# The MLP's up and down weight tiles in alternation, in a fused attention, MoE and MLP kernel on one Trainium2 core

## The chip, the core and the metric

The kernel is one launch on 1 core of a Trainium2 chip. A core has TensorE (PE, with its weight loads PEld), VectorE (DVE), ScalarE (ACT), GpSimd (POOL) and a queue for DMA issues, SyncE (SP). Each engine works through its own list of instructions in order, and waits on the others by semaphores. The metric is the device time of one execution in microseconds; it is given as the median of several runs.

## The reference

Attention with a learned position bias, then a mixture of experts with a capacity, then a dense MLP. Only the last concerns the change:

```
def _moe2_ref(x, w_in, w_out):          # x 1152x512, w_in 512x2048, w_out 2048x512
    h = x @ w_in
    g = np.maximum(0.01 * h, h)
    return (g @ w_out).astype(np.float32)

def reference(**kwargs):
    attn_out = _attn_ref(**attn_kwargs)
    B, H, S, D = attn_out.shape
    x = np.ascontiguousarray(attn_out.transpose(0, 2, 1, 3)).reshape(B * S, H * D)
    x = _moe_ref(x=x, **moe_kwargs)     # tokens over an expert's capacity give zero rows
    return _moe2_ref(x=x, **moe2_kwargs)
```

The weights `w_in` and `w_out` come as 64-bit floats.

## The kernel before

Attention runs first, unit by unit, then the routing, the experts (`big_step`, `small`) and last the dense MLP (`chunk`), which the change is about. In the runs here `chunk` is called once, as `chunk(0, True)`: 608 columns (tokens) in five groups of up to 128. A branch behind it holds further chunks.

**The weights.** The MLP's weights are 16 tiles of 128 x 1024: tiles 0 to 7 are the up matrix, 256 hidden units each, tiles 8 to 15 the down matrix, 256 hidden units each. Down tile 8+j needs the hidden units of up tile j. `PO` is the order in which the loop takes them; I call an index into it a place. Before, it is four up tiles, four down, four up, four down; the last three places, 13 to 15, are worked token group by token group behind the loop, each group's output being scaled and scattered when it is done (`emit`).

**Conversion.** A tile arrives as 64-bit floats (`conv_load`, 1 MB into a buffer `w`) and is made into a 32-bit tile `raw` by three passes on VectorE (`conv_op`, lines 689, 691 and 693), each of 128 x 1024. The passes of all tiles from place 3 on are one generator, `convs`; the loop pulls them with `next(cv, None)` at set points, and after a third pass the load of the tile two places on is issued. The tiles of the first three places are converted earlier: `conv_drip` does it inside the attention, and their results go to memory (`wsc`) and are fetched again during the experts (`DSL`).

**Splitting.** For precision each operand is a high and a low part. `wsplit` makes them from `raw`: a cast on ScalarE (line 675) and a subtraction on GpSimd (line 676, on VectorE for the last tile). At the start of place i the loop splits the tile of place i+2. A product is three matmuls.

**An up tile** (`up_half`, four times): 12 matmuls of 304 columns into one of three `g` buffers in PSUM; ScalarE's `mul` by 0.01 (line 884); VectorE's max of that and the `g` buffer (line 885), after which the buffer is free; then, called for the half before, the copy of the high part on ScalarE (line 892) and its residual on VectorE (line 893), in `split_h`. The hidden activations are `hq`.

**A down tile**: five groups of three matmuls of 512 columns, twice (`down_tok`), which is 30 matmuls into five `ac` accumulators. `split_h` is called for each first group, so that the pending last half of the up tile before is finished there. Passes are pulled at the points `DCV`.

The order of the work on each engine is the order of this code; no scheduler changes it.

Of the kernel before, what the change touches and what calls it, by code (L numbers as in the profile page):

```python
# [41 lines left out]
MOF = (0, 608)  # L42
NMC = len(MCS)
DCV = (0, 2, 4, 1)
PO = (0, 1, 2, 3, 8, 9, 10, 11, 4, 5, 6, 7, 12, 13, 14, 15)
MC = max(MCS)
XW = T + CAPB
SR1 = S + CAPB
# [26 lines left out]
def tile_attention_moe_mlp(ctx, tc, qc, kc, vc, wpk, cst, ctok, cap, wm, wo, out):  # L75
# [126 lines left out]
    def tick(k=1):  # L202
        for _ in range(k):
            while dq:
                try:
                    next(dq[0])
                    break
                except StopIteration:
                    dq.pop(0)
# [276 lines left out]
    def route_acc(b, cs):  # L486
        for c in cs:
            a = b * NCH + c
            nc.vector.tensor_tensor(out=acc[:, a + 1], in0=acc[:, a], in1=oh[:, b, c], op=ALU.add)
            yield  # L490
# [70 lines left out]
    def run(gen):  # L561
        for _ in gen:
            pass

    def scatter(b, c):
        n = 128 if c < NFULL else TAIL
        nc.gpsimd.indirect_dma_start(srt, bass.IndirectOffsetOnAxis(slots[b][0:n, c : c + 1].bitcast(U32), 0), xns.pop((b, c))[0:n], None,
                                     bounds_check=SROWS - 1, oob_is_err=False)
# [99 lines left out]
    raws, Ps, xhls, regs = [], [], [], {}  # L668
    PE, ACT, DVE, SP = ET.PE, ET.Activation, ET.DVE, ET.SP

    def wdma(src, raw):
        nc.sync.dma_start(raw, src)

    def wsplit(raw, P_, eng):
        nc.scalar.copy(P_[:, 0], raw)  # L675
        eng.tensor_tensor(out=P_[:, 1], in0=raw, in1=P_[:, 0].bitcast(F32), op=ALU.subtract)  # L676

    wsc = dr.tile([16, 128, 1024], F32, name="wsc")
    cvl = {}

    def conv_load(q, w64):
        cvl[q] = w64.bitcast(U32)
        nc.sync.dma_start(w64, wo[q].bitcast(I32).rearrange("p (f t) -> p f t", t=2))

    def conv_op(q, dst, i):
        o = dst.bitcast(U32)
        hi, lo = cvl[q][:, :, 1], cvl[q][:, :, 0]
        if i == 0:
            nc.vector.tensor_scalar(o, hi, 3, 0x3FFFFFFF, op0=ALU.logical_shift_left, op1=ALU.bitwise_and)
        elif i == 1:  # L690
            nc.vector.scalar_tensor_tensor(out=o, in0=hi, scalar=0xC0000000, in1=o, op0=ALU.bitwise_and, op1=ALU.bitwise_or)
        else:
            nc.vector.scalar_tensor_tensor(out=o, in0=lo, scalar=29, in1=o, op0=ALU.logical_shift_right, op1=ALU.bitwise_or)  # L693
# [3 lines left out]
            conv_op(q, dst, i)  # L697

    CV0 = 20
    CVA = [0, 1, 2]  # L700
    cvd = {}

    def g_w64(k):
        conv_load(CVA[k], wp.tile([128, 1024, 2], I32, name="w64g", tag="G", bufs=3))

    def conv_drip(n, slot):
        k, odd = divmod(n - CV0, 2)
        if not 0 <= k < len(CVA):
            return
# [3 lines left out]
        if i < 3:  # L713
            conv_op(CVA[k], cvd[k], i)
            tick()

    def wsrc(e, j):
        return wm[bass.ds(e, 1), j].rearrange("a p f -> p (a f)")
# [45 lines left out]
    def hooks(n):  # L764
# [28 lines left out]
        k, odd = divmod(n - CV0 - 2, 2)  # L793
        if odd == 0 and 0 <= k < len(CVA):
            nc.sync.dma_start(wsc[CVA[k]], cvd[k])
            if k + 3 < len(CVA):
                g_w64(k + 3)
# [24 lines left out]
    def tail_part(fa):  # L822
        att.close()
        mo = ctx.enter_context(tc.tile_pool(name="mo", bufs=1))
        spare = wp.tile([128, 1024], F32, name="spare", tag="bs", bufs=5)
# [28 lines left out]
        def hg(part, m, lo, n):  # L854
            o = MC * (m % 4) + lo
            return hq[2 * part + m % 8 // 4][:, o : o + n]
# [32 lines left out]
        def split_h():  # L889
            if gfh:  # L890
                gf, m, lo, n = gfh.pop()
                nc.scalar.copy(hg(0, m, lo, n), gf)  # L892
                nc.vector.tensor_tensor(out=hg(1, m, lo, n), in0=gf, in1=hg(0, m, lo, n).bitcast(F32), op=ALU.subtract)  # L893
# [13 lines left out]
        def yprep(c):  # L907
            n = MCS[c] // 2
            for lo in (0, n):
                for k in range(NP):  # L910
                    yk = y[:, k, MOF[c] + lo : MOF[c] + lo + n]
                    h = yhl[:, 0, k, lo : lo + n]
                    nc.scalar.copy(h, yk)
                    nc.vector.tensor_tensor(out=yhl[:, 1, k, lo : lo + n], in0=yk, in1=h.bitcast(F32), op=ALU.subtract)
# [64 lines left out]
        def list1():  # L979
            yield from route1b()  # L980
            yield from totals(1)
            yield from blocklist()
# [3 lines left out]
        def bval(l, i, f, engines):  # L986
            o = 3 * (NLST * l + i) + (2, 0, 1)[f]
            return nc.values_load(blk[0:1, o : o + 1], engines=engines, min_val=0, max_val=(E_N - 1, SROWS - CAPB, T - 1)[f])
# [3 lines left out]
        def load_x(base):  # L992
            for t, n in xtiles:
                nc.sync.dma_start(xr[t][0:n], srt[sl_(base + 128 * t, n), 0:DM])
# [4 lines left out]
        def load_xs(base):  # L999
            nc.sync.dma_start(xsr, srt[sl_(base, CAPS), 0:DM])  # L1000
# [13 lines left out]
        DSL = (3, 7, 12)  # L1014
        DSS = (4, 11)

        def post0(j, mm):
            s = 2 * j + mm
            if s == 0:
                run(fin_c(*fa))  # L1020
                run(route_acc(1, [NFULL]))
                scatter(1, 2)
            if s == 1:
                scatter(1, 3)
            if s == LS:
                nxt["g"] = list1()
            for _ in range(LN if s >= LS else 0):
                next(nxt["g"], None)
            if s == LE:
                run(nxt["g"])  # L1030
            if s < 2:
                wdma(wsrc(regs["e0"], 6 + s), R8[6 + s])
            if s in DSL:
                wdma(wsc[DSL.index(s)], spare)
            if s in DSS:
                wsplit(spare, Ds[DSS.index(s)], nc.vector)
            if s in (6, 8, 10, 12):
                nc.scalar.copy(y[:, s // 2 - 3], pre[:, 0:480].unsqueeze(1).to_broadcast([128, 3, 480]))
            if s == LE + 1:
                nxt["e"] = bval(0, 1, 0, [SP])  # L1040
            if s == LX:
                load_x(bval(0, 1, 1, [SP]))
                load_xs(bval(1, 0, 1, [SP]))
            for q in NXQ.get(s, ()):
                wdma(wsrc(nxt["e"], q), R8[q])
# [132 lines left out]
        def conv_start(i):  # L1178
            if i < 16:
                conv_load(PO[i], w64s[i % 2])  # L1180

        def convs():
            for i in range(3, 16):
                for o in range(3):
                    conv_op(PO[i], raws[i % 4], o)
                    if o == 2:
                        conv_start(i + 2)
                    yield
# [19 lines left out]
        def chunk(c, first):  # L1208
            w = MCS[c]
            groups = [(t, min(128, w - 128 * t)) for t in range(-(-w // 128))]  # L1210
            cv = convs()
            PP = [Ds[i] if first and i < 2 else Ps[i % 4] for i in range(16)]
            if not first:
                for i in range(3):
                    wdma(wsc[i], raws[i])
                yprep(c)
            for i in range(3, 5):
                conv_start(i)
            if not first:
                for i in range(2):  # L1220
                    wsplit(raws[i], PP[i], nc.vector)
            for i in range(13):
                if i + 2 < 16:
                    wsplit(spare if first and i == 0 else raws[(i + 2) % 4], PP[i + 2], nc.gpsimd)
                q = PO[i]
                if q < 8:
                    for g in (0, 2, 1, 3):
                        up_half(PP[i], 2 * q + g // 2, w // 2 * (g % 2), w // 2)
                        if g != 3:
                            next(cv, None)  # L1230
                else:
                    for kk in range(2):
                        for t, n in groups:
                            down_tok(PP[i], 2 * (q - 8) + kk, t, n)
                            if t == 0:
                                split_h()
                            if 2 * t + kk in DCV:
                                next(cv, None)
                if i == 5:
                    for t, n in groups:  # L1240
                        nc.sync.dma_start(idg[0:n, t], sid[MOF[c] + 128 * t : MOF[c] + 128 * t + n].bitcast(I32))
            wsplit(raws[15 % 4], PP[15], nc.vector)
            for t, n in groups:
                for i in range(13, 16):
                    for kk in range(2):
                        down_tok(PP[i], 2 * (PO[i] - 8) + kk, t, n)
                emit(t, n)
# [121 lines left out]
```

## Time and profile before

| | |
|---|---|
| median of 3 runs | 410.69 us (410.64 to 411.08) |
| the profiled execution | 410.08 us |
| its span in the trace | 408.2 us |
| TensorE busy | 377.8 us, 93% |
| VectorE busy | 308.3 us, 76% |
| ScalarE busy | 241.1 us, 59% |
| GpSimd busy | 139.3 us, 34% |
| mean granted clock of TensorE | 0.988 |

The span is the time from the first to the last instruction in the trace; the execution's own time is 1.9 us longer. Busy time is summed over the whole span and says nothing about which engine sets the pace of one stage. The ends of matmuls are modelled, so how fast TensorE goes is read from the starts of its matmuls.

### The profile page before, as it was taken

Reading aid. Unit: us, or ns where it says so; the run is one execution under the profiler, and the core shown is the slowest. Engines: PE = TensorE matmul, PEld = TensorE weight load, DVE = VectorE, ACT = ScalarE, POOL = GpSimd, SP = SyncE. Lnnn points to the kernel's source line nnn. Section 1 sums busy time; section 2 is a strip of 40 time slices with the busy share of each in tenths; the row PEclk is TensorE's granted clock in tenths of the full one; section 3 lists DMA queues with packets and bytes.
Section 4 is the critical chain, followed back from the end, with each engine's and each line's share of the span. In section 5 each row is a group of like instructions: output and inputs, shape, how many; then the busy total and the mean of one; then the engine's idle time right before and its main releaser. Section 6 shows DMA issues by size and latency. Waiting matters only on the chain. (4 is left out here: it accounts for less than half of the span.)

```text
span 408.2 us, 8432 instructions
## 1 busy us (share of the span) xinstructions
PE 377.8 (93%) x2990; PEld 313.4 (77%) x2990; DVE 308.3 (76%) x736; ACT 241.1 (59%) x519; POOL 139.3 (34%) x110
## 2 busy tenths in 40 slices
PE   4887899998899999999999989999999999899993
PEld 2245466666688888988889979998998778788872
DVE  5997989999864789799458962128899999999310
ACT  3755898898875777776664955546554222455100
POOL 1443857674200111212242115840242255222311
PEclk9998999999999999999999999999899999999998
DMA  8989599798778938788185369782343365630011
GB/s 199 335 244 325 185 315 339 263 305 260 211 215 289 346 115 258 207 271 235 35 246 190 99 208 396 256 304 100 119 159 142 105 206 205 207 106 2 16 61 51
DMA packets 34370, 82.97 MB, mean 203 GB/s; under 512 B 8491, under 2 KB 8875, under 8 KB 32272
## 3 DMA queue, kind: packets, MB, share of 16 engines
q1 hardware_dynamic: 33200, 79.88, 60.8%
q0 software_dynamic: 1120, 2.48, 1.7%
q8 instruction: 25, 0.41, 0.4%
q14 instruction: 25, 0.20, 0.1%
HBM read 60.29 MB, written 23.20 MB: 205 GB/s over the span
## 5 line engine op out<-in xcount | busy, mean ns | idle before, releaser
L345 DVE CUSTOM_DVE_ANT_0 sv<-St,bt 128x576 f32<-128x576 f32 x72 | 52.9, 750 | 31.3 <-PE St L333 20.1
L676 POOL TENSOR_TENSOR P<-raw,P 128x1024 fp32r<-128x1024 f32 x18 | 45.5, 2527 | 72.4 <-ACT P L675 55.7
L356 ACT ACTIVATE A<-sv,mx 128x576 f32<-128x576 f32 x72 | 59.4, 840 | 3.8 <-DVE mx L345 3.7
L333 PE MATMUL St<-K,Q 128*128 128x320 f32 (+1 forms) x320 | 53.8, 311 | 3.2 <-DVE mx L345 2.8
L333 PEld LDWEIGHTS St<-K,Q 128*128 128x128 f32 x320 | 44.3, 191 | 15.0 <-issue 9.8
L182 PE MATMUL pb<-Gt,WP 128*32 128x272 f32 (+17 forms) x352 | 43.7, 496 | 11.7 <-DVE Gt L165 8.2
L273 POOL TENSOR_TENSOR Q<-qr,Q 128x256 fp32r<-128x256 f32 x22 | 17.0, 773 | 100.2 <-ACT Q L265 62.1
L165 DVE TENSOR_SCALAR Gt<-WL,bp 128x432 f32<-128x432 f32 (+17 forms) x101 | 48.4, 540 | 0.1
L675 ACT CAST P<-raw 128x1024 fp32r<-128x1024 f32 x27 | 28.3, 1048 | 28.8 <-DVE raw L693 22.2
L366 PE MATMUL pt<-CS,A 128*128 128x128 f32 x288 | 42.4, 288 | 1.7 <-ACT A L356 0.8
L376 ACT COPY AT<-pt 128x512 f32<-128x512 f32 x40 | 23.4, 585 | 30.4 <-PE pt L366 30.1
L366 PEld LDWEIGHTS pt<-CS,A 128*128 128x128 f32 x288 | 38.7, 207 | 2.6 <-ACT A L356 1.3
L169 POOL TENSOR_SCALAR Gt<-WL,bp 128x528 f32<-128x528 f32 (+12 forms) x17 | 34.5, 2031 | 9.3 <-PE pb L182 9.2
L182 PEld LDWEIGHTS pb<-Gt,WP 128*32 128x32 f32 x352 | 13.0, 110 | 30.0 <-DVE Gt L165 14.4
L403 PE MATMUL xp<-AT,V 128*64 128x128 f32 x512 | 35.0, 279 | 0.0
L193 ACT ACTIVATE bs<-pb,CS 128x288 f32<-128x288 f32 (+53 forms) x60 | 27.4, 505 | 12.0 <-PE pb L182 7.5
L403 PEld LDWEIGHTS xp<-AT,V 128*64 128x64 f32 x512 | 27.3, 136 | 9.1 <-issue 8.8
L860 PE MATMUL g<-yhl,P 128*128 128x304 f32 x96 | 30.3, 316 | 3.1 <-DVE gfa L885 3.1
L1197 PE MATMUL ac<-P,hq 128*128 128x512 f32 (+1 forms) x80 | 31.5, 394 | 0.0
L1195 PE MATMUL ac<-P,hq 128*128 128x512 f32 (+1 forms) x80 | 31.5, 394 | 0.0
L1196 PE MATMUL ac<-P,hq 128*128 128x512 f32 (+1 forms) x80 | 31.5, 393 | 0.0
L893 DVE TENSOR_TENSOR hq<-gfa,hq 128x304 fp32r<-128x304 f32 x32 | 29.0, 907 | 1.4 <-ACT hq L892 1.4
(322 smaller groups left out, 907.1 us busy)
## 6 DMA issues: line engine op xcount, KB each, us to landing
bt<-scr SPq DMA_DIRECT2D x24, 576.0 KB, 4.7
w<-wo SPq DMA_DIRECT2D x13, 1024.0 KB, 5.1
scr<-bs SPq DMA_DIRECT2D x36, 295.5 KB, 5.0
raw<-wm SPq DMA_DIRECT2D x14, 512.0 KB, 7.6
w<-wm SPq DMA_DIRECT2D x10, 512.0 KB, 6.5
srt<-pre SPq DMA_DIRECT2D x6, 771.0 KB, 7.8
qr<-qc SPq DMA_DIRECT2D x16, 256.0 KB, 6.2
kr<-kc SPq DMA_DIRECT2D x12, 288.0 KB, 6.9
```

The lines of the kernel that those rows point to most:

```text
L165: nc.vector.tensor_scalar(G, src, bp[:, g : g + 1], 0.0, op0=ALU.add, op1=ALU.max)
L169: nc.gpsimd.tensor_scalar(G, src, bp[:, g : g + 1], 0.0, op0=ALU.add, op1=ALU.max)
L182: nc.tensor.matmul(pb[32 * q : 32 * q + 32, 0 : hi - lo], W2, gs[:, q, lo:hi], start=True, stop=True)
L333: nc.tensor.matmul(St[:, o + lo : o + hi], Q[:, h - 2 * p, w, :], K[:, h - 2 * p, lo:hi], start=n == 0, stop=n == len(seq) - 1)
L345: nc.vector.tensor_tensor_reduce(out=sv, in0=St, in1=bt[:, jb], scale=-0.125, scalar=3.0e38, op0=ALU.add, op1=ALU.min, accum_out=mx)
L356: nc.scalar.activation(A[:, :, j], sv, AF.Exp, bias=mx, scale=-1.0, accum_out=rs[:, col : col + 1])
L366: nc.tensor.transpose(pt[:, 128 * t : 128 * t + 128], A[:, 128 * t : 128 * t + 128, j], ident)
L403: nc.tensor.matmul(xp[64 * j : 64 * j + 64, p, :], w, a, start=t == 0, stop=t == NFULL)
L676: eng.tensor_tensor(out=P_[:, 1], in0=raw, in1=P_[:, 0].bitcast(F32), op=ALU.subtract)
L1195: nc.tensor.matmul(ps, hh, wh, start=k == 0, stop=False)
L1196: nc.tensor.matmul(ps, hh, wl, start=False, stop=False)
L1197: nc.tensor.matmul(ps, hl, wh, start=False, stop=k == F2 // 128 - 1)
```

## The change

The order `PO` becomes up, up, down, and then mostly up and down in turn: 0, 1, 8, 2, 9, 3, 10, 4, 11, 5, 6, 12, 7, 13, 14, 15. The first three tiles, which are converted early, follow it (0, 1, 8 in place of 0, 1, 2). An up tile now pulls two conversion passes, behind its first and second half, and a third one only at places 0, 1 and 10; a down tile pulls four, as before. Since the loop now ends with an up tile (place 12), `split_h` is called once behind it.

```
-PO = (0, 1, 2, 3, 8, 9, 10, 11, 4, 5, 6, 7, 12, 13, 14, 15)
+PO = (0, 1, 8, 2, 9, 3, 10, 4, 11, 5, 6, 12, 7, 13, 14, 15)
...
-    CVA = [0, 1, 2]
+    CVA = PO[:3]
...
             if s in DSL:
-                wdma(wsc[DSL.index(s)], spare)
+                wdma(wsc[PO[DSL.index(s)]], spare)
...
                 for i in range(3):
-                    wdma(wsc[i], raws[i])
+                    wdma(wsc[PO[i]], raws[i])
...
                     for g in (0, 2, 1, 3):
                         up_half(PP[i], 2 * q + g // 2, w // 2 * (g % 2), w // 2)
-                        if g != 3:
+                        if g != 3 and (g != 1 or i in (0, 1, 10)):
                             next(cv, None)
...
+            split_h()
             wsplit(raws[15 % 4], PP[15], nc.vector)
```

Here is what stands in VectorE's list from place 2 on, behind the end of the second up tile. L885 is the max, L893 the residual, L689, L691 and L693 are the three passes. Before:

```order
L885 TENSOR_TENSOR gfa<-g_3194,gfa 128x304
L893 TENSOR_TENSOR hq_3179<-gfa,hq_3177 128x304
L885 TENSOR_TENSOR gfa<-g_3195,gfa 128x304
L893 TENSOR_TENSOR hq_3179<-gfa,hq_3177 128x304
L689 TENSOR_SCALAR raw<-w_3176 128x1024
L885 TENSOR_TENSOR gfa<-g_3193,gfa 128x304
L893 TENSOR_TENSOR hq_3180<-gfa,hq_3178 128x304
L691 SCALAR_TENSOR_TENSOR raw<-w_3176,raw 128x1024
L885 TENSOR_TENSOR gfa<-g_3194,gfa 128x304
L893 TENSOR_TENSOR hq_3180<-gfa,hq_3178 128x304
L693 SCALAR_TENSOR_TENSOR raw<-w_3176,raw 128x1024
```

And now, the down tile of place 2 and the up tile of place 3:

```order
L885 TENSOR_TENSOR gfa<-g_3194,gfa 128x304
L893 TENSOR_TENSOR hq_3179<-gfa,hq_3177 128x304 x2
L689 TENSOR_SCALAR raw<-w_3176 128x1024
L691 SCALAR_TENSOR_TENSOR raw<-w_3176,raw 128x1024
L693 SCALAR_TENSOR_TENSOR raw<-w_3176,raw 128x1024
L689 TENSOR_SCALAR raw<-w_3175 128x1024
L885 TENSOR_TENSOR gfa<-g_3195,gfa 128x304
L691 SCALAR_TENSOR_TENSOR raw<-w_3175,raw 128x1024
L885 TENSOR_TENSOR gfa<-g_3193,gfa 128x304
L893 TENSOR_TENSOR hq_3180<-gfa,hq_3178 128x304
L693 SCALAR_TENSOR_TENSOR raw<-w_3175,raw 128x1024
```

The three passes of a tile, which alternated with the halves of an up tile, now stand in one block behind the residual of the last half, and the first pass of the next tile with them; the next up tile keeps two passes between its halves.

ScalarE's list at the same place: L675 is the cast of a weight tile, L884 the `mul`, L892 the copy. Before:

```order
L675 CAST P<-raw 128x1024
L884 ACTIVATE gfa<-g_3195 128x304
L892 CAST hq_3177<-gfa 128x304
L884 ACTIVATE gfa<-g_3193 128x304
L892 CAST hq_3178<-gfa 128x304
```

And now:

```order
L892 CAST hq_3178<-gfa 128x304
L675 CAST P<-raw 128x1024
L892 CAST hq_3178<-gfa 128x304
L675 CAST P<-raw 128x1024
L884 ACTIVATE gfa<-g_3194 128x304
L884 ACTIVATE gfa<-g_3195 128x304
L892 CAST hq_3177<-gfa 128x304
```

In a down place the copy of the last half stands alone between two casts; in an up place two `mul` follow the cast.

The end of VectorE's list in the loop, where the last tile's low half (L676) and the scaling of the output (L1202) stand. Before:

```order
L885 TENSOR_TENSOR gfa<-g_3194,gfa 128x304
L893 TENSOR_TENSOR hq_3180<-gfa,hq_3178 128x304 x2
L676 TENSOR_TENSOR P_3174<-raw,P_3174 128x1024
L1202 TENSOR_SCALAR osb_4073<-ac_3200,idg 128x512
L1202 TENSOR_SCALAR osb_4075<-ac_3202,idg 128x512
```

And now:

```order
L693 SCALAR_TENSOR_TENSOR raw<-w_3176,raw 128x1024
L885 TENSOR_TENSOR gfa<-g_3193,gfa 128x304
L893 TENSOR_TENSOR hq_3180<-gfa,hq_3178 128x304
L885 TENSOR_TENSOR gfa<-g_3194,gfa 128x304
L893 TENSOR_TENSOR hq_3180<-gfa,hq_3178 128x304 x2
L676 TENSOR_TENSOR P_3174<-raw,P_3174 128x1024
```

The rows alike are these: before, they belong to up tile 7 and are followed on TensorE by the whole down tile 12; now up tile 7 is the last thing in the loop, and the last pass of tile 15 (L693) stands within it.

## Rows read from the trace of the kernel before

**Rows 1.** Busy time by stretch: start:end, length, each engine, PEclk, DMA share, GB/s.

```profile
299.90:380.50 80.60, 77.54 (x440) 67.78 (x439) 76.92 (x90) 32.25 (x64) 28.75 (x11) 1.00 0.39 131
```

**Rows 2.** Timeline of TensorE: start us, length us, engine, line, tile, [idle before <-releaser].

```profile
299.89 0.30 PE L860 MATMUL g<-yhl,P 128*128 128x304 f32 x1
...
343.01 0.30 PE L860 MATMUL g<-yhl,P 128*128 128x304 f32 x1
...
343.29 0.30 PE L862 MATMUL g<-yhl,P 128*128 128x304 f32 x1
...
373.58 0.39 PE L1195 MATMUL ac<-P,hq 128*128 128x512 f32 x1
...
380.51 0.40 PE L1195 MATMUL ac<-P,hq 128*128 128x512 f32 x1
```

**Rows 3.** Waits of TensorE from 299.9 to 381 us: total, times, longest.

```profile
PE g L860 <- DVE gfa L885: 3.1, 4, 0.9
```

**Rows 4.** Timeline of ScalarE over one up tile.

```profile
303.08 1.05 ACT L675 CAST P<-raw 128x1024 fp32r<-128x1024 f32 x1 [1.12 <-DVE raw L693]
304.03 0.42 ACT L884 ACTIVATE gfa<-g 128x304 f32<-128x304 f32 x1
...
311.44 1.05 ACT L675 CAST P<-raw 128x1024 fp32r<-128x1024 f32 x1 [1.13 <-DVE raw L693]
```

**Rows 5.** Timeline of VectorE over the same up tile.

```profile
304.48 0.47 DVE L885 TENSOR_TENSOR gfa<-g,gfa 128x304 f32<-128x304 f32 x1 [0.73 <-ACT gfa L884]
304.87 2.07 DVE L893 TENSOR_TENSOR hq<-gfa,hq 128x304 fp32r<-128x304 f32 x1
306.87 0.68 DVE L689 TENSOR_SCALAR raw<-w 128x1024 uint32<-128x1024 uint32 x1
307.47 0.46 DVE L885 TENSOR_TENSOR gfa<-g,gfa 128x304 f32<-128x304 f32 x1
...
308.24 1.22 DVE L691 SCALAR_TENSOR_TENSOR raw<-w,raw 128x1024 uint32<-128x1024 uint32 x1
309.37 0.46 DVE L885 TENSOR_TENSOR gfa<-g,gfa 128x304 f32<-128x304 f32 x1
```

**Rows 6.** Timeline of GpSimd, one subtraction during the down tiles.

```profile
328.01 2.91 POOL L676 TENSOR_TENSOR P<-raw,P 128x1024 fp32r<-128x1024 f32 x1 [4.67 <-ACT P L675]
```

**Rows 7.** Timeline of VectorE during the down tiles.

```profile
323.58 0.68 DVE L689 TENSOR_SCALAR raw<-w 128x1024 uint32<-128x1024 uint32 x1
324.30 1.23 DVE L691 SCALAR_TENSOR_TENSOR raw<-w,raw 128x1024 uint32<-128x1024 uint32 x1
325.56 1.23 DVE L693 SCALAR_TENSOR_TENSOR raw<-w,raw 128x1024 uint32<-128x1024 uint32 x1
...
328.68 3.31 DVE L693 SCALAR_TENSOR_TENSOR raw<-w,raw 128x1024 uint32<-128x1024 uint32 x1
```

**Rows 8.** Timeline of all engines, first down tile behind up tiles.

```profile
319.81 1.05 ACT L675 CAST P<-raw 128x1024 fp32r<-128x1024 f32 x1 [1.12 <-DVE raw L693]
...
320.76 0.44 ACT L892 CAST hq<-gfa 128x304 fp32r<-128x304 f32 x1
...
320.94 2.39 POOL L676 TENSOR_TENSOR P<-raw,P 128x1024 fp32r<-128x1024 f32 x1 [5.96 <-PE ac L1197]
...
321.24 2.42 DVE L893 TENSOR_TENSOR hq<-gfa,hq 128x304 fp32r<-128x304 f32 x1 [0.75 <-ACT hq L892]
```

**Rows 9.** Timeline of VectorE, the low half of the last weight tile.

```profile
380.34 1.21 DVE L676 TENSOR_TENSOR P<-raw,P 128x1024 fp32r<-128x1024 f32 x1
```

**Rows 10.** Stretches as in rows 1, and TensorE's last matmul in the timeline.

```profile
284.00:292.00 8.00, 7.48 (x41) 7.18 (x41) 7.29 (x14) 5.17 (x13) 2.38 (x1) 0.79 0.59 231
402.00:404.00 2.00, 0.00 (x0) 0.00 (x0) 0.00 (x0) 0.33 (x1) 0.93 (x1) 1.00 0.03 8
...
401.21 0.40 PE L1197 MATMUL ac<-P,hq 128*96 128x512 f32 x1
```

**Rows 11.** DMA issues: queue, operation, count, KB each, median us to landing.

```profile
w<-wo SPq DMA_DIRECT2D x13, 1024.0 KB, 5.1
```

## The prediction

> **What bounds the kernel now.** The part that changes is the first call of `chunk`, the last stage, so I read it in three steps. First the stretches: from 299.9 to 380.5 us TensorE shows 77.5 of 80.6 us busy, but VectorE shows 76.9 as well [rows 1]. A busy matmul row is modelled, so I next read starts. The third up tile starts at 299.89, the second group of four up tiles runs from 343.01 to 373.58, one down tile from 373.58 to 380.51, which is 6.93 us or 0.231 per matmul (30 of them); two up matmuls are 0.28 apart, so an undisturbed up tile of 48 takes 6.72 [rows 2]. Between 299.89 and 380.51 lie six up and five down tiles: 6 x 6.72 + 5 x 6.93 = 75.0 us. They took 80.6, so TensorE stood 5.6 us. Its waits name one releaser, the max on VectorE that frees a `g` buffer [rows 3]. That is all this part could give back. The third step is who makes VectorE late.
>
> In an up tile the chain is read from three engines. ScalarE's cast of the tile two places on starts at 303.08; ScalarE is free for the first `mul` 0.95 later, at 304.03 [rows 4]; the max follows 0.45 behind it, at 304.48 [rows 5]. The next cast starts at 311.44, 8.36 later, against TensorE's 6.72 [rows 4]. VectorE's own steps, start to start: max 0.39, max and residual together 0.77, pass 1 0.60, pass 2 (and 3, the same kind) 1.13 [rows 5]. That is 4 x 0.77 + 2.86 = 5.94 of the 8.36; the rest is a residual that took 2.07 where a max of its size takes 0.47, and idle time [rows 5].
>
> The reason for the 2.07 is plainest where ScalarE hands over to GpSimd. Cast at 319.81, copy of the pending half at 320.76, GpSimd's subtraction from 320.94 for 2.39, VectorE's residual at 321.24, after 0.75 of idleness, for 2.42: it ends at 323.66, 0.33 after GpSimd [rows 8]. A pass is held the same way: GpSimd ran from 328.01 to 330.92 [rows 6], and pass 3, started at 328.68, ended at 331.99, 1.07 after it [rows 7]. The max at 304.48 reads PSUM and is not held [rows 5]. So every weight tile puts about 2.4 us of GpSimd in VectorE's way, whatever the order.
>
> **The change part by part.** No instruction is added or removed but one empty call of `split_h`. The early tiles change only in which tile is fetched and converted (8 in place of 2), at the same size: nothing. The loads `w<-wo` take 5.1 us from issue to landing [rows 11]; each is issued when a conversion ends, and one whole conversion (7 us or more, below) lies before it is needed: nothing, unless a conversion takes under 5.1. The `idg` loads keep their place 5 on the DMA queue and are read only at the end. Places 0 and 1 keep their passes, so the cast at 303.08 stands where it is, now at the head of a down tile (place 2).
>
> The working is the chain cast, GpSimd, VectorE, next cast. I call a place's cast c, and the four half groups of an up tile A to D.
>
> *Down place.* GpSimd runs from c+1.13 to c+3.53 [rows 8]. The residual of D, first in VectorE's queue, is ready at c+1.43 and so always meets it: it ends at c+3.86. Behind it stand four passes. Pass 1 starts at c+3.78, and in a row the passes take 0.72, 1.26 and 1.23 [rows 7], so the tile is ready at c+6.99. At 311.44 a cast started 0.08 after its pass 3 (309.37 + 0.77 + 1.22) [rows 4, 5]; the next cast is therefore at **c+7.07**. The fourth pass, 0.7 long, fits ahead of the next max.
>
> *Up place.* Max A starts at c+0.95+0.45 = c+1.40. Pass 2 is next, at c+1.79, while GpSimd works until c+3.53; it ends at c+4.60. A pass 2 that is held has no row: the bounds are 0.33 after GpSimd (the residual) and 1.07 (pass 3). I take 1.07, since pass 3 has the same shape and the same two operands. Then max B and residual A 0.77, pass 3 1.13, max C, which ends at c+6.89. ScalarE's queue has the copy of C (0.44, of which I take 0.4) ahead of the next cast: **c+7.29**.
>
> A pair of tiles thus takes 14.36 us on this chain, and TensorE needs 6.72 + 6.93 = 13.65. Alternation does even out the work, but each place now pays its handover: in the down place VectorE idles about 0.7 before the residual of D, in the up place about 0.9 before max A, and no passes are queued to fill it. Before, in the four down tiles in a row, only the first had such a residual, and the passes ran on behind one another [rows 7, 8].
>
> The walk: place 2 has its cast at 303.08, place 3 at 310.15, place 4 at 317.44, then 14.36 a pair: place 9 at 353.23, place 10 at 360.52. Place 10 is an up tile behind an up tile: residual D held to c+3.86, then pass 1 0.60, max and residual 0.77, pass 2 1.13, 0.77, pass 3 1.22, next cast at c+8.35 = 368.87 (place 11, down), place 12 at 375.94.
>
> TensorE has three `g` buffers, so half D of an up tile waits for max A, to c+1.40+0.47. In place 12 that is 377.81; D takes 12 x 0.14 = 1.68, so the last three tiles start at about 379.5, 1.0 earlier than now (380.51).
>
> *The end.* Now the last tile's low half is done at 380.34 + 1.21 = 381.55 [rows 9], and TensorE wants it after the 12 matmuls of tiles 13 and 14, at 380.51 + 2.77 = 383.28: covered by 1.7 us. The change puts up tile 7 directly ahead, and takes that cover away. Max D ends at 375.94 + 7.66 = 383.60, the copy 0.4, the cast 1.05, the low half 1.21: 386.3. TensorE wants it at 382.3 and waits 4.0, less one matmul (0.23) that needs only the high half: 3.8.
>
> Sum: -1.0 + 3.8 = +2.8 us. The profiled execution took 410.08 us, 1.9 more than its span of 408.2, and would become 412.9; the median of the runs is 0.6 above it, so **413.5**.
>
> **The clock in the last wait.** From 284 to 292 the granted clock was 0.79 on average, because after a stretch of few short matmuls it stood at the lower of its two levels (1.2 GHz); that costs 0.21 x 8 = 1.7 us. On the other side TensorE's last matmul ends at 401.61 and the clock is still whole from 402 to 404 [rows 10]. The last wait lies between: about 4 us with one matmul in it. The Trainium skill, TensorE: Matmul & The Clock Gate, section HAM oscillation, says that a wait between bursts of matmuls puts the array back to its low clock, so that the next burst begins slow; by that rule the sum would be 1.7 us more, by the second row it stays.
>
> **The rivals.** *The clock falls in the last wait:* as above, +2.8 + 1.7 = 415.2. For it speaks that the wait is emptier than the stretch before 286; against it the clock of 402 to 404.
>
> *The evening-out works (faster).* Counting VectorE's work alone, a pair is 4 x 0.77 + 2 x 2.86 + two holds of 1.6 = 12.0 us, under TensorE's 13.65. If the handovers hide behind passes, no `g` buffer is waited for, and the loop ends at 299.89 + 75.0 = 374.9. Behind D then come mul and max 0.9, copy 0.4, cast 1.05, low half 1.2: ready at 378.5, wanted at 374.9 + 2.77 = 377.7, which leaves 0.8 less one matmul. -5.6 + 0.6 = -5.0: 405.7. The point from which it decides is a pair under 13.65 on the chain. For it: the work itself; against it: the handover rows, where neither queue has anything else to run [rows 8].
>
> *It nets out.* If the held pass 2 ends early (the bound of 0.33, so 0.74 less in each of five up places), the chain is level with TensorE (13.62 a pair): place 12 has its cast at 373.0, up tile 7 ends at 373.0 + 1.87 + 1.68 = 376.5, the low half is there at 386.3 - 3.7 = 382.6, wanted at 379.3, and -4.0 + 3.1 = -0.9, or 409.8. With three quarters of that 0.74 it is 410.7.
>
> **How the numbers follow.** Forecast 413.5, 0.45: everything in it has a row, but for pass 2. An error of 0.2 a pair makes about 1 us by the end, so its own range is 412.4 to 414.6. Clock falls, 415.2: 0.33. Evening-out: 0.12. Nets out: 0.10. A measurement of this kernel tells 0.2% (0.8 us) from no change; so faster 0.13, same 0.09, slower 0.78. The range goes from 411.2, which takes in part of netting out, to 416.0, above the case with the clock, and leaves out the evening-out and little more.
>
> **What would show it.** Right: casts alternately about 7.1 and 7.3 us apart from 303.08 on; in each down place one residual of about 2.4 us behind 0.7 of idleness; in each up place a pass 2 of about 2.9; the last three tiles starting near 379.5; one wait of 2 to 4 us there, released by VectorE's low half, near 386. Wrong: casts under 6.8 apart on average, no wait for `g`, up tile 7 done near 375. A wait of a pass on `w<-wo`, or of a down matmul on a residual, would be something that I have not priced. A granted clock under 1 behind the last wait decides between the first two cases.

## The result: 415.57 us, slower by 1.1%

| | before | after |
|---|---|---|
| median (lowest to highest), 6 runs each on one chip | 410.69 us (409.63 to 412.52) | 415.57 us (412.15 to 417.95) |
| ratio after to before, 95% interval | | 1.0108 (1.0059 to 1.0157) |
| profiled execution, its span | 410.08, 408.2 us | 416.57, 414.7 us |
| first matmul of the MLP (L860) | 284.50 us | 285.74 us |
| from there to the end of the span | 123.7 us | 129.0 us |

The head of the page of the profile of after, the busy time of each engine, and the granted clock in 40 slices (a 9 is 0.9 of full speed or more):

```profile
span 414.7 us, 8437 instructions
...
PE 381.5 (92%) x2990; PEld 315.9 (76%) x2990; DVE 308.4 (74%) x736; ACT 240.8 (58%) x519; POOL 136.7 (33%) x110
...
PEclk9999699998999999999999999998999999999699
```

Two things stand in the clock row. The third digit from the end is a 6 and is the subject of all that follows. The fifth digit is a 6 too, and it is not the change's: it lies near 45 us, before the MLP, a second profile of the same kernel (e8 below) does not have it and its MLP began at 283.20, and a profile of the kernel before with one edit (e11) has it. So I compare the two traces from the MLP's first matmul on, where after took 5.3 us longer (129.0 against 123.7); in e8 it is 129.0 again.

The stretch that answers to [rows 1], from the third weight tile to the last three (columns: window, length, then busy time and count of PE, PEld, DVE, ACT, POOL; granted clock, share of the DMA engines, GB/s):

```profile
301.10:380.80 79.70, 76.66 (x440) 67.66 (x439) 70.80 (x81) 29.35 (x59) 26.37 (x11) 1.00 0.40 133
```

It is 79.7 us long against 80.6. VectorE's busy time in it fell by 6 us, but the time that TensorE needs did not change. VectorE's work as a whole is the same (308.4 against 308.3 us): what left this stretch now stands behind it, over the last three tiles. The chain that sets the pace, on ScalarE (start, duration, engine, line, operation; in brackets the idle time before it and what ended it):

```profile
304.34 1.05 ACT L675 CAST P<-raw 128x1024 fp32r<-128x1024 f32 x1 [1.13 <-DVE raw L693]
...
311.42 1.05 ACT L675 CAST P<-raw 128x1024 fp32r<-128x1024 f32 x1 [5.69 <-DVE raw L693]
...
318.69 1.04 ACT L675 CAST P<-raw 128x1024 fp32r<-128x1024 f32 x1
```

The casts are 7.08 and 7.27 us apart. GpSimd and VectorE between them, each in its own list:

```profile
312.55 2.39 POOL L676 TENSOR_TENSOR P<-raw,P 128x1024 fp32r<-128x1024 f32 x1 [4.67 <-ACT P L675]
319.81 2.40 POOL L676 TENSOR_TENSOR P<-raw,P 128x1024 fp32r<-128x1024 f32 x1 [4.87 <-ACT P L675]
```

```profile
311.25 0.69 DVE L689 TENSOR_SCALAR raw<-w 128x1024 uint32<-128x1024 uint32 x1
312.82 0.47 DVE L885 TENSOR_TENSOR gfa<-g,gfa 128x304 f32<-128x304 f32 x1 [0.89 <-ACT gfa L884]
313.22 2.80 DVE L691 SCALAR_TENSOR_TENSOR raw<-w,raw 128x1024 uint32<-128x1024 uint32 x1
...
320.11 2.43 DVE L893 TENSOR_TENSOR hq<-gfa,hq 128x304 fp32r<-128x304 f32 x1 [0.66 <-ACT hq L892]
...
386.22 1.23 DVE L676 TENSOR_TENSOR P<-raw,P 128x1024 fp32r<-128x1024 f32 x1 [0.47 <-ACT P L675]
```

In the up place VectorE idles 0.89, and pass 2 then takes 2.80, because GpSimd is in its subtraction until 314.94; the pass ends 1.08 behind it. In the down place VectorE idles 0.66 and the residual takes 2.43, as in [rows 8]. The last row answers to [rows 9]: the low half of tile 15 now ends at 387.45. TensorE's waits from 300 to 392 us (total, times, longest):

```profile
PE g L860 <- DVE gfa L885: 2.9, 5, 1.2
...
PE ac L1195 <- ACT P L675: 2.4, 1, 2.4
...
PE ac L1196 <- DVE P L676: 0.5, 1, 0.5
```

The waits for `g` of [rows 3] are still there, 2.9 us in place of 3.1, and the other two are new. Where they stand, on TensorE:

```profile
380.83 0.39 PE L1195 MATMUL ac<-P,hq 128*128 128x512 f32 x1
...
383.40 0.40 PE L1197 MATMUL ac<-P,hq 128*128 128x512 f32 x1
386.24 0.79 PE L1195 MATMUL ac<-P,hq 128*128 128x512 f32 x1 [2.44 <-ACT P L675]
387.50 0.79 PE L1196 MATMUL ac<-P,hq 128*128 128x512 f32 x1 [0.47 <-DVE P L676]
...
388.52 0.63 PE L1195 MATMUL ac<-P,hq 128*128 128x512 f32 x1
388.95 0.63 PE L1196 MATMUL ac<-P,hq 128*128 128x512 f32 x1
...
392.77 0.40 PE L1196 MATMUL ac<-P,hq 128*128 128x512 f32 x1
```

The matmul at 387.50 is the 14th of the last three tiles; at 0.231 each it would have started at 380.83 + 13 x 0.231 = 383.84. The wait cost 3.7 us. Behind it the matmuls start 0.43 apart instead of 0.23, and the windows show why (columns as above):

```profile
384.00:386.00 2.00, 0.00 (x0) 0.00 (x0) 1.62 (x4) 1.65 (x3) 0.00 (x0) 0.98 0.00 0
386.00:388.00 2.00, 1.29 (x2) 0.79 (x3) 1.23 (x1) 0.19 (x1) 0.00 (x0) 0.50 0.00 0
388.00:390.00 2.00, 2.00 (x6) 1.52 (x6) 0.00 (x0) 0.00 (x0) 0.00 (x0) 0.50 0.00 0
390.00:392.00 2.00, 2.00 (x7) 1.51 (x6) 0.00 (x0) 0.69 (x1) 0.99 (x1) 0.50 0.00 0
392.00:394.00 2.00, 2.00 (x9) 1.59 (x8) 0.00 (x0) 0.00 (x0) 0.00 (x1) 0.81 0.34 131
```

The clock is whole until the end of the empty stretch, is at its lower level (0.50, 1.2 GHz) from 386 to 392, and is whole again within the next row. From the first matmul of the last three tiles to the end of the span after took 33.9 us, before 27.7 (408.2 - 380.51). Of the 6.2, 3.7 are the wait; 2.5 are left for the clock. The starts say the same: from 387.50 to 392.77 there are twelve steps, which took 5.27 us and would take 2.77 at 0.231 each, so 2.5 less.

### The profile page after: what moved, and what is told of

Its sections match the earlier page's. It is cut to its first block, busy times and chain, and to the rows that moved or that the text cites. A ratio compares the mean times of both kernels' runs of the same rounds, so it can differ in the third digit from the quotient of the medians.

```text
span 414.7 us, 8437 instructions
## 1 busy us (share of the span) xinstructions
PE 381.5 (92%) x2990; PEld 315.9 (76%) x2990; DVE 308.4 (74%) x736; ACT 240.8 (58%) x519; POOL 136.7 (33%) x110
## 5 line engine op out<-in xcount | busy, mean ns | idle before, releaser
L676 POOL TENSOR_TENSOR P<-raw,P 128x1024 fp32r<-128x1024 f32 x18 | 43.1, 2396 | 74.2 <-ACT P L675 62.9
L182 PE MATMUL pb<-Gt,WP 128*32 128x272 f32 (+17 forms) x352 | 44.8, 525 | 13.3 <-DVE Gt L165 8.1
L675 ACT CAST P<-raw 128x1024 fp32r<-128x1024 f32 x27 | 28.3, 1047 | 37.9 <-DVE raw L693 31.2
L366 PE MATMUL pt<-CS,A 128*128 128x128 f32 x288 | 41.5, 284 | 1.6 <-ACT bs L193 1.4
L403 PE MATMUL xp<-AT,V 128*64 128x128 f32 x512 | 36.8, 288 | 0.0
L403 PEld LDWEIGHTS xp<-AT,V 128*64 128x64 f32 x512 | 28.7, 142 | 10.0 <-issue 9.8
L1195 PE MATMUL ac<-P,hq 128*128 128x512 f32 (+1 forms) x80 | 32.8, 409 | 2.4 <-ACT P L675 2.4
L1196 PE MATMUL ac<-P,hq 128*128 128x512 f32 (+1 forms) x80 | 32.6, 407 | 0.5 <-DVE P L676 0.5
L860 PE MATMUL g<-yhl,P 128*128 128x304 f32 x96 | 29.7, 310 | 3.0 <-DVE gfa L885 2.9
L1197 PE MATMUL ac<-P,hq 128*128 128x512 f32 (+1 forms) x80 | 32.5, 406 | 0.0
L893 DVE TENSOR_TENSOR hq<-gfa,hq 128x304 fp32r<-128x304 f32 x32 | 27.8, 867 | 3.6 <-ACT hq L892 3.5
```

What stands on the lines that cost most here:

```text
L182: nc.tensor.matmul(pb[32 * q : 32 * q + 32, 0 : hi - lo], W2, gs[:, q, lo:hi], start=True, stop=True)
L366: nc.tensor.transpose(pt[:, 128 * t : 128 * t + 128], A[:, 128 * t : 128 * t + 128, j], ident)
L403: nc.tensor.matmul(xp[64 * j : 64 * j + 64, p, :], w, a, start=t == 0, stop=t == NFULL)
L1195: nc.tensor.matmul(ps, hh, wh, start=k == 0, stop=False)
L1196: nc.tensor.matmul(ps, hh, wl, start=False, stop=False)
L1197: nc.tensor.matmul(ps, hl, wh, start=False, stop=k == F2 // 128 - 1)
```

## The experiments

**My theory:** conversions are paced by the chain "cast, GpSimd, VectorE, next cast", because a subtraction on GpSimd holds VectorE's operations; alternation lets VectorE idle at every handover, and up tile 7, directly ahead of the last three tiles, takes the cover from the conversion of tile 15. The wait there then drops the clock. **Rivals:** the mixed order itself costs TensorE time; the later beginning of the MLP belongs to the change; the clock fell for some other reason than the wait. "Before" is the kernel before on the same chip. A length of the MLP comes from one profile, and carries an uncertainty that the medians average out: at its head the clock is low in some executions (0.79 over 284 to 292) and whole in others. One kernel profiled both ways (e2 and e10) took 117.5 with it whole and 118.95 with it low. Where the chain sets the pace this does not show: the cast of place 2 stands 18.6 us behind the MLP's first matmul in before, after, e1 and e5, with 0.79 at the head in the first two and 1.00 in the others.

**e1, the conversion pass ahead of the residual of D.** The down place's first pass fills the idle time.

```diff
                         for t, n in groups:
                             down_tok(PP[i], 2 * (q - 8) + kk, t, n)
-                            if t == 0:
-                                split_h()
                             if 2 * t + kk in DCV:
                                 next(cv, None)
+                            if t == 0:
+                                split_h()
```

> The changed kernel, with the first pass of a down place pulled ahead of the pending residual in place of behind it; same instructions. My theory: VectorE has an idle 0.66 us there, behind the cast, and pass 1 (0.7 us) fits into it, so the cast of the up place comes 0.7 us earlier in each of five down places. A pair then takes 13.6 us, level with TensorE; the low half of the last tile comes 3.6 us earlier, and the time is 409.5 to 410 us if the clock holds in the last wait, some 2 us more if it falls (about 3 us of waiting are left). Rival: only GpSimd's hold matters, and the pass merely changes places with the residual: no change, about 415.5 us, casts still 7.1 and 7.3 us apart.

Measured: 411.18 us (12 runs), before 410.81, ratio 1.0023 (0.9996 to 1.0049). VectorE's list in the first such place:

```profile
303.51 0.68 DVE L689 TENSOR_SCALAR raw<-w 128x1024 uint32<-128x1024 uint32 x1
304.33 2.44 DVE L893 TENSOR_TENSOR hq<-gfa,hq 128x304 fp32r<-128x304 f32 x1 [0.15 <-ACT hq L892]
306.70 1.21 DVE L691 SCALAR_TENSOR_TENSOR raw<-w,raw 128x1024 uint32<-128x1024 uint32 x1
```

The idle time is 0.15 in place of 0.66, and the casts stand at 302.90, 309.26, 316.53 and 322.97: 6.36, 7.27 and 6.44 apart, so 0.6 to 0.7 less in a down place and the same in an up place. The last three tiles start 91.8 us behind the MLP's first matmul instead of 95.1. The swap of two calls gave back about four fifths of the loss (0.2% is left of 1.1%), which the rivals do not explain. The last wait stayed (2.5 for the high half, 0.8 for the low one), and the clock fell there too, for half as long (0.83 over 380 to 384, 0.75 over 384 to 388: 3.4 us at the lower level). The MLP took 124.8 us, 4.2 less than in after: 3.3 are the earlier start of the last three tiles, and about 0.9 the shorter fall of the clock.

**e2 and e3, the subtraction on VectorE.** e2 makes this edit in the changed kernel, e3 in the kernel before. GpSimd then does no subtraction of the loop.

```diff
-                    wsplit(spare if first and i == 0 else raws[(i + 2) % 4], PP[i + 2], nc.gpsimd)
+                    wsplit(spare if first and i == 0 else raws[(i + 2) % 4], PP[i + 2], nc.vector)
```

> The changed kernel, with the low halves of all weight tiles subtracted on VectorE in place of GpSimd; nothing left out. My theory: each place puts 1.1 us more on VectorE, but nothing holds it and the subtraction fills the idle time at the handover. Down place about 5.9 us from cast to cast at the earliest, up place about 6.2, so a pair needs 12.1 us on this chain and TensorE's 13.65 is the bound: no wait for g buffers, a last wait under 1 us, no fall of the clock: about 406 us. Rival: the alternation itself costs TensorE (weights or buffers changing at each tile), whoever does the low halves: then it stays several us slower than the kernel before with the same edit, and up and down tiles take more than 6.7 and 6.9 us.

> The kernel before, with the same edit (low halves on VectorE in the loop). My theory: an up tile's chain falls from 8.4 to about 7.2 us, so TensorE's 5.6 us of waiting in the loop shrink to 0 to 1.5 us: 405 to 407 us, the same as the changed kernel with this edit within 1 us, since with the hold gone the order of the tiles no longer matters. Rival (the alternation itself costs): this one is 4 us or more faster than the changed kernel with the edit. A second rival: alternation does even out the work once the hold is gone: this one is 1 to 2 us slower than it.

Measured: e2 403.61 us, ratio 0.9843 (0.98 to 0.9886); e3 404.88, ratio 0.9864 (0.9819 to 0.9909); 4 runs each. An up place on VectorE in e2, and all that TensorE waited for from 300 to 392 us:

```profile
308.36 1.23 DVE L676 TENSOR_TENSOR P<-raw,P 128x1024 fp32r<-128x1024 f32 x1 [0.57 <-ACT P L675]
309.50 0.47 DVE L885 TENSOR_TENSOR gfa<-g,gfa 128x304 f32<-128x304 f32 x1
309.88 1.22 DVE L691 SCALAR_TENSOR_TENSOR raw<-w,raw 128x1024 uint32<-128x1024 uint32 x1
```

```profile
PE ac L1196 <- DVE P L676: 0.7, 1, 0.7
```

The subtraction takes 1.23 here instead of 2.39 on GpSimd, and pass 2 takes 1.22 instead of 2.80. The hold cost 1.6 us in an up place, and 2.0 in a down place (a residual of 2.43 instead of 0.46). VectorE is here the better place for the work even though it was the busier engine. The first casts are 5.91 and 6.50 apart, under TensorE's 6.93 and 6.72; further on a pair takes 13.6 us (5.86 and 7.78), which is TensorE's own 13.65. No wait for `g` is left, and 0.7 of the last one. Both kernels came out under the time that I had expected, e2 by 2.4 us.

**e10 and e11, the same two kernels again**, in one batch, since the 1.3 us between e2 and e3 could have been the order or the clock at the head (whole in e2, 0.79 in e3).

> The changed kernel with the low halves on VectorE, once more with more rounds, beside the next run. My theory (with no hold, the order of the tiles decides nothing): the same as the kernel before with that edit within 0.8 us. Rivals: alternation evens out the work, then it is 1.2 us faster, as in the first pair of runs; alternation costs TensorE, then slower.

> The kernel before with the low halves on VectorE, once more. My theory: 403.5 to 405 us, and within 0.8 us of the changed kernel with that edit; in its first profile the clock was low at the start of the MLP for some 3 us, in the other's not, which can be their difference. Rival (evening out): 404.9 us again, and 1.2 us over the other.

Measured: 405.96 us, ratio 0.9889 (0.9855 to 0.9924), and 405.73, ratio 0.9885 (0.9855 to 0.9915); 6 runs each; both had 0.79 at the head, and their MLPs took 118.95 and 118.8. e2's kernel thus differed by 2.4 us from one batch to the other, and e11 is 0.7 over what I had expected; the pair to compare is the one in one batch. Without GpSimd in VectorE's way the order of the tiles makes no difference that these runs can tell: the medians are 0.2 us apart and so are the MLPs. The rival by which alternation itself costs TensorE several us is out.

**e4 and e6, the cover given back.** Tiles 13 and 14 are multiplied for the first three token groups (e4) or two (e6) before tile 15 is touched.

```diff
+            for t, n in groups[:3]:
+                for i in range(13, 15):
+                    for kk in range(2):
+                        down_tok(PP[i], 2 * (PO[i] - 8) + kk, t, n)
             for t, n in groups:
-                for i in range(13, 16):
+                for i in range(13 if t > 2 else 15, 16):
```

> The changed kernel, with the end in another order: tiles 13 and 14 of the first three token groups, then tile 15 of these three, then the last two groups as before; same matmuls. My theory: the chain in the loop stays as it is (casts 7.1 and 7.3 us apart, last three tiles starting 0.9 us earlier than before the change), but 36 matmuls (8.3 us) now cover the wait for tile 15, so the wait of about 3.8 us and the fall of the clock behind it are gone: 409.8 us, 0.9 under the kernel before. Rival: the loss is in the loop and not at its end, or the clock falls whatever is done: 412 us or more.

> As the run with the covered end, but tiles 13 and 14 of only the first two token groups go ahead of tile 15, so that the outputs come in less of a bunch: in that run the scatters of the outputs stood 3.5 us apart and the last one ended 2.9 us later than TensorE's last matmul asked for. My theory: 24 matmuls (5.6 us) cover the wait but for about 1 us, the scatters catch up by the last group, the clock holds: 4 us under the changed kernel, about 411 us. Rival: the loss at the end is the scatters' own, however they are spread: 413 us, as with three groups.

Measured: e4 412.99 us, ratio 1.0051 (1.0019 to 1.0082); e6 411.39, ratio 1.0018 (0.9989 to 1.0048); 12 runs each. e6 is clear of the changed kernel in its own batch (e8 below, 1.0137, 1.0086 to 1.0188), e4's interval overlaps that of after. The clock stayed at 1.00 from 380 to 392 in both. e4 missed its number by 3 us and by the time alone lies with the rival (412 or more), but its trace does not: TensorE's last matmul ended 116.2 us behind the MLP's first, 0.9 earlier than in the kernel before (117.1), which is what the theory said. GpSimd's list, which issues the output scatters, shows where the 3 us went:

```profile
391.68 1.00 POOL L1205 DMA_INDIRECT out<-osb,idg  x1 [11.15 <-ACT osb L1204]
395.22 0.98 POOL L1205 DMA_INDIRECT out<-osb,idg  x1 [2.54 <-issue]
398.67 0.97 POOL L1205 DMA_INDIRECT out<-osb,idg  x1 [2.47 <-issue]
402.14 0.97 POOL L1205 DMA_INDIRECT out<-osb,idg  x1 [2.50 <-issue]
405.74 0.94 POOL L1205 DMA_INDIRECT out<-osb,idg  x1 [2.62 <-issue]
```

The first scatter comes at 391.68 (before 385.86), and the others follow 3.45 to 3.6 us apart with nothing else to wait for, so the last is issued 3.9 us after TensorE's last matmul ended (401.83). In the kernel before that is 1.0 us. With two groups (e6) it is 1.3: the last scatter is issued at 402.80, and TensorE ended at 401.51.

**e7, a filled wait.** In the last wait TensorE runs 14 more matmuls of 512 columns; their result is not read.

```diff
             for t, n in groups:
                 for i in range(13, 16):
+                    if t == 0 and i == 15:
+                        for r in range(14):
+                            nc.tensor.matmul(gs[gi[0] % 3], hg(0, 12, 0, 128), PP[14][:, 0, 0:512], start=True, stop=True)
```

> The changed kernel with 14 extra matmuls of 512 columns, whose result nobody reads, in the last wait (3.2 us of about 3.8). My theory: they change nothing but the clock; it stays whole behind the wait where it fell for some 6 us in the changed kernel's profile, so the time is 2 us under that kernel where its clock falls: about 413 us. Rival: the clock's fall has nothing to do with the wait, or costs nothing: no change, about 415 us.

**e8, the changed kernel again**, in the batch of e7.

> The changed kernel as it is, on the same chip as the runs beside it. Both theories: 414 to 416 us, casts 7.1 and 7.3 us apart, and a last wait of about 3.8 us. By mine the clock falls behind that wait in most executions, and the stretch ahead of the MLP takes as long as in the kernel before: the 1.2 us by which the MLP began later in its first profile should not come again of necessity. Rival: that later beginning belongs to the change.

Measured: e7 413.24 us (12 runs), ratio 1.0084 (1.0057 to 1.011); e8 415.05 (6 runs), ratio 1.0137 (1.0086 to 1.0188). TensorE gets tile 15's low half at 385.01 in e7 and at 384.96 in e8. The stretch in which the last wait ends, in e7 and then in e8:

```profile
384.00:392.00 8.00, 7.72 (x34) 5.96 (x33) 1.71 (x2) 0.69 (x1) 1.30 (x2) 1.00 0.08 33
```

```profile
384.00:386.00 2.00, 1.54 (x4) 0.84 (x4) 0.91 (x1) 0.00 (x0) 0.00 (x0) 0.50 0.00 0
386.00:388.00 2.00, 2.00 (x6) 1.61 (x5) 0.00 (x0) 0.50 (x1) 0.00 (x0) 0.50 0.00 0
388.00:390.00 2.00, 2.00 (x6) 1.52 (x6) 0.00 (x0) 0.19 (x1) 0.99 (x1) 0.50 0.00 0
390.00:392.00 2.00, 2.00 (x10) 1.61 (x9) 0.00 (x0) 0.00 (x0) 0.00 (x0) 0.93 0.34 131
```

Matmuls that do nothing useful make the kernel 1.8 us shorter by the medians and 2.4 by the MLP's length (126.6 against 129.0, the clock at the head 0.79 to 0.80 in both). The two intervals overlap, so the medians alone would not settle it; the clock of the two traces does, 1.00 against 0.50 with tile 15 at hand at the same time. So it was the empty wait that dropped the clock, and 1.8 to 2.4 us are its price; the wait itself is left in e7. The later beginning of the MLP in after did not come again in e8 (283.20).

**e5, the order alone.** The new order of the tiles with the old rule for passes.

```diff
-                        if g != 3 and (g != 1 or i in (0, 1, 10)):
+                        if g != 3:
```

> The changed kernel with the old rule for the passes: three behind every up tile's halves and four in a down tile, so the new order of the tiles alone. My theory: the conversion then runs ahead by one pass a pair, so passes are queued where VectorE idles at the handovers; the chain falls from 14.4 us a pair to about 13.1 and less, under TensorE's 13.65, and the last place has no passes left, so the low half of the last tile comes early too: 407 to 409.5 us, no long last wait, faster than the kernel before by 1 to 3 us. Rival: the order of the tiles is itself what costs, and how the passes lie changes nothing: 414 to 416 us.

Measured: 411.15 us (12 runs), ratio 1.0006 (0.9979 to 1.0033), MLP 123.6. Better than after, so the order alone does not do the harm; the change's rule for the passes has to come with it. But the 407 to 409.5 us that I expected did not come. VectorE's list in e5, and TensorE's wait for `g` from 285 to 382 us:

```profile
340.10 3.29 DVE L693 SCALAR_TENSOR_TENSOR raw<-w,raw 128x1024 uint32<-128x1024 uint32 x1
...
348.48 5.03 DVE L893 TENSOR_TENSOR hq<-gfa,hq 128x304 fp32r<-128x304 f32 x2
...
361.87 0.69 DVE L689 TENSOR_SCALAR raw<-w 128x1024 uint32<-128x1024 uint32 x1 [0.45 <-DMA w<-wo]
...
373.75 3.42 DVE L691 SCALAR_TENSOR_TENSOR raw<-w,raw 128x1024 uint32<-128x1024 uint32 x1
```

```profile
PE g L860 <- DVE gfa L885: 4.4, 3, 2.1
```

With its idle time filled, VectorE runs ahead until a pass or a pair of residuals meets two subtractions on end (5.03 for two), once even until it waits for a load. The holds come back in other places; TensorE waits 4.4 us for `g`.

**e9, both cures.** e2's and e6's edits together.

> The changed kernel with the low halves on VectorE and with tiles 13 and 14 of the first two token groups ahead of tile 15: both edits that helped. My theory: TensorE is the bound all through the loop, and the last wait that is left there (about 1.1 us in the profile with the low halves on VectorE) is covered as well, so 0.5 to 1 us less than with the first edit alone, if the bunched scatters cost nothing: 402.6 to 403.3 us. Rival: the scatters set the end once the wait is gone: no gain, 403.5 us or more.

Measured: 405.0 us (6 runs), ratio 0.9879 (0.9843 to 0.9915). In the same batch e2's kernel took 405.96 (e10), so the better cover is worth 1 us at most, inside the spread (403.85 to 407.12). The MLPs of the two profiles, both with 0.79 at the head, are 118.3 and 118.95 long, which fits the 0.7 of the last wait, and no wait of TensorE is left from 300 to 392. My number was about 2 us too low, because it was worked out from e2's 403.61, and the same kernel took 405.96 in this batch; the kernel before was not slower in it (410.01 against 410.81).

## Why the prediction held, and what was off

The time was in the range and on the forecast side; the point was 2.1 us low, because I gave the higher chance to the case without the fall of the clock. The 0.2% that I said a measurement could tell was too small: the interval is half a percent to either side. Point by point:

- **The chain.** Forecast: casts 7.07 behind a down place's cast, 7.29 behind an up place's, 8.35 at place 10. Measured: 7.08, 7.27, and 8.36 (361.69 to 370.05). The bound that I had to choose, a held pass 2 that ends 1.07 after GpSimd, came out at 1.08. e1 showed that the idle time costs, by filling it, and e2 that the hold does, by removing it. The Trainium skill, SBUF — State Buffer, section SBUF: two separate sides, says that VectorE and GpSimd share one pair of ports, which a GpSimd instruction, or a VectorE instruction with two inputs in SBUF, holds as an exclusive lock to its end; the trace agrees, with pass 2 at 2.80 beside GpSimd and 1.22 without it.
- **The start of the last three tiles.** Forecast 1.0 earlier than before. Measured from the MLP's first matmul: 380.83 - 285.74 = 95.1 against 380.51 - 284.50 = 96.0, so 0.9 earlier.
- **The last wait.** Forecast 3.8, measured 3.7; the low half ended 1.2 us later by the clock of the trace than the 386.3 forecast, which the later beginning of the MLP (1.24) accounts for. The sign that I gave, one wait released by the low half, came as two: 2.4 us for the high half (ScalarE's cast), then 0.5 for the low one. The working has the high half as well, as the one matmul that it sets off, and the end is the same.
- **The sum without the clock.** Forecast +2.8. e7, which has the wait but not the fall, measured a ratio of 1.0084 (1.0057 to 1.011), or 2.3 to 4.5 us.
- **The term that was mis-sized: the clock in the last wait.** I priced it at 1.7 from the stretch 284 to 292, where the clock was low for 3.4 us, and held it for less likely, because it stayed whole behind TensorE's last matmul [rows 10]. That row was read too short. It ends 2.4 us behind the last matmul, where the wait was to be 3.8, and the next stretch of the same trace, in which TensorE does nothing either, has the clock fallen:

```profile
404.00:408.20 4.20, 0.00 (x0) 0.00 (x0) 0.00 (x0) 0.00 (x0) 0.00 (x0) 0.66 0.15 46
```

Read to its end, the kernel before spoke for the fall. The size was low too. In after the clock was at its lower level for about 6.8 us (0.04 + 1.0 + 1.0 + 1.0 + 0.38 us of whole clock are missing in the five windows above, and the lower level misses half, so times 2), twice the 3.4 us of the stretch that I priced by. Some 5 of them had matmuls 0.43 us apart, and it cost 1.8 (medians) to 2.5 us. In e8 it fell in the same place. The Trainium skill, TensorE: Matmul & The Clock Gate, section HAM oscillation — how this bites in real kernels, says that waits between bursts bring the array back to its low clock; the trace agrees, with 0.50 behind a wait of 3.7 us and 1.00 in e7, where it was filled.

- **The rivals.** The evening-out has its time (405.7) only where the hold is gone: e10 at 405.96, and then e11 has it without the change. Netting out asked for a pass 2 that ends 0.33 after GpSimd; it ended 1.08 after it.

What stays open: why the clock was low twice as long in after as in e1, whose last wait was about as long (2.5 and 0.8); why scatters that are ready together stand 3.5 us apart; and how the spread of after's runs, with mean granted clocks of 0.974 to 0.988, divides between the several places where the clock falls.

## What to carry to other kernels

When two engines hold each other up, don't count busy time but the chain from handover to handover: evening out the work of the held engine gained nothing here while the handovers stayed, and moving the holding instruction onto the held engine gained 1.1 to 1.6% here, with or without the new order. Look at what stands directly ahead of the last stretch: a conversion that was covered before can come to stand bare, and a wait of 3.7 us there cost half to two thirds as much again through the clock. Regrouping the tail to hide a wait loses part of its gain if the outputs then bunch up: about 3 us with three groups here.

## What I had not expected of the hardware

- After a wait of 3.7 us the clock stayed at 0.50 for some 6.8 us although dense matmuls were running for 5 of them; in e1 it was 3.4.
- Scatters of the output that are ready together leave GpSimd's queue 3.45 to 3.6 us apart, about 1.0 of it busy and 2.5 shown as issue.
- Two residuals on end behind two subtractions of GpSimd took 5.03 us, where two unheld ones take about 0.9 (0.46 each in the same list).
